# Two paddings of 128 bytes in SBUF, which put the two operands of the large matmuls half of 256 bytes apart

## The chip, the cores and the metric

The kernel runs on one core of one Trainium2 chip. The metric is device time in microseconds (us) for one launch; lower is better. Three runs of the kernel before took 962.54, 964.48 and 963.08 us, with a median of 963.08 us.

## The reference, cut to what matters

Input and output are one sequence of 2048 tokens with 640 channels, in float32. Two blocks follow each other, each with a layer norm whose scale, shift and gate are rows of a small modulation product.

```
mod = silu(c) @ w_mod                      # six rows of 640
h = layernorm(x) * (1 + ca) + sa
x = x + ga * (conv(h, K) + h * Dskip)      # K: 2048 taps per channel, from 192 complex modes
h = layernorm(x) * (1 + cb) + sb
x = x + gb * ((h @ w_gate) * (h @ w_up)) @ w_down   # 640 -> 1536 -> 640
```

The first block is a long convolution, which the kernel computes through Fourier transforms written as matmuls. The second is the gated product, and the change is about its operands.

## The kernel before, in words

The first half, up to about 500 us, builds the taps of the convolution (sine, cosine and exponential tables that VectorE multiplies and TensorE contracts, lines 745 to 760), transforms taps and input (lines 782 to 937), and multiplies the spectra. Its order is written out by hand in the table `SCHED`. Its tiles lie in the pools `pk`, `pk1`, `kconst`, `f16` and `fp`, whose memory is given back when they are done.

The second half is the gated product over four blocks of 512 tokens. It takes the given-back memory for two pools, `wp` from the left end of SBUF and `gp` from the right, in which almost every tile has one place for the whole half. The blocks come in two pairs. In a pair, the products with `w_gate` and `w_up` for two token blocks are formed from sums and differences of operands, so that fewer products are needed (`y_1` to `z_2`, `x_1`, `x_2`), for twelve slices of 128 hidden units. Then `down` (line 1455) multiplies the result with `w_down`, for one token block after the other.

To keep precision, each float32 operand v is split by `hilo` into a high part, which ScalarE rounds to the float32r type, and a low part, which VectorE computes as v minus the high part (line 992). Each product is then three matmuls: high with high, low with high, high with low. So every large matmul has float32r operands.

- Line 1028, in `prod`: the stationary operand (the one that is loaded into the array first) is a block of 128 columns of a weight tile (`wsgh`, `wsgl`, `wth`, `wtl`, `wsuh`, `wsul`); the moving operand is 512 columns of an activation tile (`hh1`, `hl1`, `hh2`, `hl2`, `sh`, `sl`). The program has 1266 of these; line 1162 (`u_gate`) has 30 more of the same form.
- Line 1455, in `down`: here the stationary operand is a block of 128 columns of an activation tile (`sh`, `sl`, `hh2`, `hl2`, or one of the four `e`), and the moving operand is a weight tile's first 384 or last 256 columns (`wsgh`, `wsgl`), in turn. The program has 576 of each.

Each matmul loads its own weights, and the array can take the next weights while the present matmul streams.

Where the tiles lie: every tile of `wp` and `gp` is a multiple of 256 bytes long in each partition, and in the compiled layout every one of them starts 224 bytes past a multiple of 256. Blocks of 128 float32 columns are 512 bytes, 512 columns 2048 bytes, and 384 columns 1536 bytes, so each operand of lines 1028, 1162 and 1455 also starts 224 bytes past a multiple of 256, moving and stationary alike. `wp` is allocated in the order `gbr`, `xb0`, `xb1`, `wga`, `wgb`, `wur`, `wsgh`, `wsgl`, `st0`, `st1`, `hr`, and then `hh1`, `hl1`, `a5` to `a9` and `e`. `gp` is allocated as one list at its opening (lines 1334 to 1338), from low to high addresses: `a10` to `a14`, `s6`, `z`, `s67`, `hh2`, `hl2`, `sh`, `sl`, then `tf`, `wth`, `wtl`, `wsuh`, `wsul`, and other `a` tiles; its upper end is fixed at the end of SBUF. Between the end of `wp` (byte 106208) and the start of `gp` (byte 106464) 256 bytes are free.

`hr` (line 1063) holds small statistics of the layer norm and is used up to column 44 of its 64.

Of the kernel before, what the change touches and what calls it, by code (L numbers as in the profile page):

```python
# [10 lines left out]
F32 = mybir.dt.float32  # L11
# [8 lines left out]
P = 128  # L20
# [109 lines left out]
def tile_kernel(ctx: ExitStack, tc: tile.TileContext, I, out):  # L130
# [49 lines left out]
    def rstd(mv, rs, nm, v, y, ps=None):  # L180

        if ps is not None:
            m = mv.shape[1]
            v, t = ps[:, 0:m], ps[:, 32 : 32 + m]
            V.tensor_scalar(v, mv[:, :, 1], EPS, None, op0=OP.add)
            act(y, v, AF.Sqrt)
            V.reciprocal(rs, y)
            V.tensor_tensor(v, v, rs, op=OP.mult)
            V.tensor_tensor(v, v, rs, op=OP.mult)
            V.tensor_scalar(v, v, -0.5, 1.5, op0=OP.mult, op1=OP.add)  # L190
            V.tensor_tensor(t, v, rs, op=OP.mult)
            V.tensor_tensor(rs, v, rs, op=OP.mult)
            V.scalar_tensor_tensor(nm, t, -1.0, mv[:, :, 0], op0=OP.mult, op1=OP.mult)
            return
        V.tensor_scalar(v, mv[:, :, 1], EPS, None, op0=OP.add)
        act(y, v, AF.Sqrt)
        V.reciprocal(rs, y)
        V.tensor_tensor(y, rs, rs, op=OP.mult)
        V.tensor_tensor(y, y, v, op=OP.mult)
        V.tensor_scalar(y, y, -0.5, 1.5, op0=OP.mult, op1=OP.add)  # L200
        V.tensor_tensor(rs, rs, y, op=OP.mult)
        V.scalar_tensor_tensor(nm, mv[:, :, 0], -1.0, rs, op0=OP.mult, op1=OP.mult)
# [751 lines left out]
    FIRST, SMALL = {}, []  # L954
# [105 lines left out]

    def head_r(tb, st):
        if not SMALL:
            SMALL.append(wp.tile([P, 64], F32, name="hr"))
        mv = SMALL[0][:, 0:8].rearrange("p (i s) -> p i s", s=2)
        rs, nm, rv, ry = (SMALL[0][:, j : j + 4] for j in (16 + 4 * (tb % 2), 24 + 4 * (tb % 2), 32, 40))
        for i in range(4):
            V.bn_aggr(mv[:, i, :], st[:, i])
        rstd(mv, rs, nm, rv, ry)
        HN[tb] = (rs, nm)
# [44 lines left out]
    def u_ln(tb):  # L1114

        st = head_st(tb)
        need(1, "xr", tb, 0)
        head_b(tb, st, range(NB - 2))
        yield
        need(NB - 1, "d", tb)  # L1120
        head_b(tb, st, (NB - 2,))
        yield
        need(NB, "d", tb)
        head_b(tb, st, (NB - 1,))
        head_r(tb, st)
        mark("ln", tb)
        if tb:
            yield
            head_i(1, range(3))
            yield  # L1130
            x, (rs, nm) = XB[1][:, 3, :], HN[1]
            G.tensor_scalar(x, x, rs[:, 3:4], nm[:, 3:4], op0=OP.mult, op1=OP.add)
# [148 lines left out]
    for t in range(3 * NK + 24):  # L1281
        for i in range(3):
            due(3 * t + i)
        if t == 3 * NK + 1:
# [3 lines left out]
            wp = ctx.enter_context(tc.tile_pool(name="wp", bufs=1, reuse_waits="tile"))  # L1288
# [44 lines left out]
    H2, SX = ("hh2", "hl2"), ("sh", "sl")  # L1333
    for n, sh_, dt_, b_ in ([(f"a{j}", [P, 512], F32, 1) for j in range(10, 15)] + [(n, [P, 512], F32, 1) for n in TMP]
                            + [(n, [P, 3, 512], F32R, 1) for n in H2] + [(n, [P, 9, 512], F32R, 1) for n in SX]
                            + [("tf", [P, 8, P], F32, 1), ("wth", [P, 8, P], F32R, 2), ("wtl", [P, 8, P], F32R, 2), ("wsuh", [P, 4, P], F32R, 2),
                               ("wsul", [P, 4, P], F32R, 2)] + [(f"a{j}", [P, 512], F32, 1) for j in (*range(5), *range(15, 24))]):
        FIRST[n] = gp.tile(sh_, dt_, name=n, bufs=b_)
# [167 lines left out]
    def stats(tb, i0):  # L1506
        if i0 == 0:
            ST[tb] = head_st(tb)
        head_b(tb, ST[tb], range(NB), range(i0, i0 + 2))
        if i0:  # L1510
            head_r(tb, ST.pop(tb))
# [113 lines left out]
```

## Time and profile before

| what | before |
|---|---|
| median of three runs | 963.08 us |
| the profiled execution, its own time | 962.99 us |
| its span, from the first to the last instruction | 961.2 us |
| mean granted TensorE clock | 0.975 |
| TensorE matmuls (PE), records and busy time | 11070, 864.6 us |
| weight loads (PEld), records and busy time | 11070, 715.9 us |
| VectorE (DVE), ScalarE (ACT), GpSimd (POOL) busy | 760.1, 569.7, 567.8 us |

The page lists each engine's busy time, then a strip of 40 slices of the span, then the chain of work that ended last. A matmul's record runs from its start to the time its last result is through the pipeline, so records of matmuls that follow each other overlap, and a sum of their durations is more than the time they take. The time that one of them takes in a stream is the distance between starts: the step. The timeline merges neighbouring records of one group; its columns are the start, the time from the first start to the last end, the engine, the line, the tiles (output, then inputs), the shapes and the count.

### The profile page before, as it was taken

To read this page: it belongs to the slowest core of one execution; us is meant where nothing else is said; L and a number is where in the kernel's file an instruction comes from. 1 tells how busy PE (TensorE), PEld (TensorE's weight loads), DVE (VectorE), ACT (ScalarE), POOL (GpSimd) and SP (SyncE) were. 2 spreads that over 40 slices of the span, in tenths; PEclk is the share of its full clock that TensorE was granted. 3 is DMA by queue.
4 is the path that set the end of the run, shared out by engine and by line. 5 is a ranking of instruction groups with operands and counts; after the bars stand their busy time and mean duration, and the time that the engine had idled before them with its cause. 6 is when DMAs were issued, how large, how long until landed. Compare 5 with 4: busy or idle time off the path is not lost.

```text
span 961.2 us, 26424 instructions
## 1 busy us (share of the span) xinstructions
PE 864.6 (90%) x11070; PEld 715.9 (74%) x11070; DVE 760.1 (79%) x1328; ACT 569.7 (59%) x1022; POOL 567.8 (59%) x419
## 2 busy tenths in 40 slices
PE   2778876898798699989889999999999999999998
PEld 1565655676575467678567888899998888889998
DVE  8988678888989988897899877696677877688452
ACT  6889988887987888864773322235555322224330
POOL 5999999799799999950126767631031544451000
PEclk9977999899999889999999999999999999999999
DMA  9487565444565644558953454255536222212241
GB/s 301 152 267 263 150 217 191 134 132 126 145 181 147 186 130 144 161 175 266 254 168 89 130 192 139 80 192 164 193 137 219 84 83 82 83 55 83 83 165 55
DMA packets 141320, 148.94 MB, mean 155 GB/s; under 512 B 8208, under 2 KB 119568, under 8 KB 139792
## 3 DMA queue, kind: packets, MB, share of 16 engines
q1 hardware_dynamic: 139904, 145.80, 48.6%
q8 instruction: 87, 1.43, 0.6%
q10 hardware_dynamic: 1296, 1.44, 0.5%
q14 instruction: 33, 0.27, 0.1%
HBM read 108.36 MB, written 38.86 MB: 153 GB/s over the span
## 4 chain that ended last, share of the span: by engine, by line
PE 49%; DVE 4%; ACT 1%; DMA 1%; issue 1%; DVEq 0%; SPq 0%; ACTq 0%
PE pa L1028 28%; PE pa L1455 17%; PE psg L1028 1%; DMA wga<-B_w_gate 1%; DVE sl L992 1%; PE psg L1108 0%; PE psg L1455 0%; DVE a L1147 0%; PE psg L1162 0%; DVE xb L1468 0%; ACT wsgh L135 0%; PE psfa L887 0%; DVE f16a L873 0%; DVE f16a L874 0%; PE psfb L887 0%
## 5 line engine op out<-in xcount | busy, mean ns | idle before, releaser
L649 POOL TENSOR_TENSOR EQ<-LQ,RH 128x1536 f32<-128x1536 f32 x40 | 124.2, 3106 | 2.2 <-DVE QtB L731 2.1
L135 ACT ACTIVATE z<-pa 128x512 f32<-128x512 f32 x24 | 14.4, 599 | 168.0 <-PE pa L1028 115.0
L992 DVE TENSOR_TENSOR wsgl<-wga,wsgh 128x640 fp32r<-128x640 f32 x72 | 69.8, 973 | 45.6 <-ACT wsgh L135 45.6
L135 ACT ACTIVATE wsgh<-wga 128x640 fp32r<-128x640 f32 x72 | 52.3, 732 | 63.4 <-PE pa L1455 34.1
L1399 POOL TENSOR_TENSOR z<-z,s 128x512 f32<-128x512 f32 x24 | 34.2, 1423 | 88.4 <-DVE s L1398 88.4
L1004 POOL TENSOR_TENSOR tf<-wur,wgb 128x256 f32<-128x256 f32 x24 | 18.8, 784 | 97.0 <-DVE wtl L992 58.9
L649 POOL TENSOR_TENSOR EP<-LP,RH 128x768 f32<-128x768 f32 x40 | 65.7, 1651 | 11.8 <-DVE PtB L731 11.8
L1455 PE MATMUL pa<-wsgh,sh 128*128 128x384 f32 (+1 forms) x295 | 68.6, 311 | 0.0
L1455 PE MATMUL pa<-wsgl,sh 128*128 128x384 f32 (+1 forms) x295 | 68.2, 310 | 0.0
L1455 PE MATMUL pa<-wsgh,sl 128*128 128x384 f32 (+1 forms) x295 | 68.2, 310 | 0.0
L649 POOL TENSOR_TENSOR Pha<-LH,DH 128x1536 int32<-128x1536 int32 (+1 forms) x21 | 62.4, 2971 | 1.8 <-ACT tra L135 1.6
L649 POOL TENSOR_TENSOR Phb<-LH,DH 128x1536 int32<-128x1536 int32 x20 | 62.3, 3113 | 0.0
L992 DVE TENSOR_TENSOR wtl<-tf,wth 128x256 fp32r<-128x256 f32 (+1 forms) x72 | 58.8, 844 | 0.0
L731 DVE TENSOR_TENSOR QtA<-tra,EQ 128x1024 f32<-128x1024 f32 x44 | 51.9, 1215 | 7.7 <-ACT tra L135 4.8
L1397 DVE TENSOR_TENSOR s<-pa,s 128x512 f32<-128x512 f32 x24 | 16.6, 690 | 42.8 <-PE pa L1028 37.8
L731 DVE TENSOR_TENSOR QtA<-trb,EQ 128x1024 f32<-128x1024 f32 x36 | 42.7, 1217 | 9.7 <-ACT trb L135 5.5
L760 PE MATMUL kg<-QtB,PtB 64*32 64x64 f32 x2560 | 46.1, 222 | 4.7 <-issue 2.7
L760 PEld LDWEIGHTS kg<-QtB,PtB 64*32 64x32 f32 x2560 | 39.1, 110 | 12.5 <-issue 6.4
L1028 PE MATMUL pa<-sh,wtl 128*128 128x512 f32 x144 | 44.7, 391 | 0.8 <-DVE wtl L992 0.8
L1455 PEld LDWEIGHTS pa<-wsgh,sl 128*128 128x128 f32 x295 | 45.3, 188 | 0.0
L1455 PEld LDWEIGHTS pa<-wsgl,sh 128*128 128x128 f32 x295 | 45.3, 188 | 0.0
L1455 PEld LDWEIGHTS pa<-wsgh,sh 128*128 128x128 f32 x295 | 45.3, 188 | 0.0
(653 smaller groups left out, 2854.7 us busy)
## 6 DMA issues: line engine op xcount, KB each, us to landing
wga<-wdg SPq DMA_DIRECT2D x24, 640.0 KB, 4.2
wga<-B_w_gate SPq DMA_DIRECT2D x12, 640.0 KB, 5.8
wgb<-B_w_gate SPq DMA_DIRECT2D x24, 320.0 KB, 3.3
wur<-B_w_up SPq DMA_DIRECT2D x24, 320.0 KB, 4.0
xb<-x2d SPq DMA_DIRECT2D x6, 1280.0 KB, 7.1
t_ti<-w_mod SPq DMA_DIRECT2D x3, 1600.0 KB, 9.5
t_tw<-w_mod SPq DMA_DIRECT2D x3, 1600.0 KB, 9.8
WD<-Wa SPq DMA_DIRECT2D x8, 512.0 KB, 4.1
```

Source lines behind the costliest of these rows:

```text
L135: return S.activation(o, i, f, **kw)
L649: G.tensor_tensor(o.rearrange("p x (h l) -> p x h l", l=8), lo.unsqueeze(2).to_broadcast([P, rows, nh, 8]), hi.rearrange("p h x -> p x h") ...
L731: V.tensor_tensor(t, tr, e.unsqueeze(1).to_broadcast([P, 2, R, 32]), op=OP.mult)
L760: PE.matmul(kg[j * 32 : j * 32 + 32, dd, :], PtB[lo : lo + 64, c, r, :], QtB[lo : lo + 64, c, r, :], start=False, stop=dd == 7 and c == 1, ...
L992: V.tensor_tensor(lo, v, hi, op=OP.subtract)
L1004: G.tensor_tensor(t[:, 0:2], u[:, 0:2], g[:, 0:2], op=OP.subtract)
L1028: PE.matmul(ps, w[a][:, k], x[b][:, l], start=n == 0 and m == 0, stop=n == 2 and m == len(ks) - 1)
L1397: V.tensor_tensor(S67[i], ps, S6[i], op=OP.add)
L1399: G.tensor_tensor(ZT[i], ZT[i], S67[i], op=OP.add)
L1455: PE.matmul(ACC[tb][t][c], x[:, ts], w[:, cs], start=st, stop=f == NF - 1 and n == 2 and (one or t % 2 == 1))
```

## The change: what it does

`hr` becomes 96 columns wide, that is 384 bytes instead of 256, and a tile `gap` of 128 bytes, which nothing reads or writes, is put between `sl` and `tf` in the list of `gp`. No instruction is added, removed or moved.

```
     def head_r(tb, st):
         if not SMALL:
-            SMALL.append(wp.tile([P, 64], F32, name="hr"))
+            SMALL.append(wp.tile([P, 96], F32, name="hr"))
...
     for n, sh_, dt_, b_ in ([(f"a{j}", [P, 512], F32, 1) for j in range(10, 15)] + [(n, [P, 512], F32, 1) for n in TMP]
                             + [(n, [P, 3, 512], F32R, 1) for n in H2] + [(n, [P, 9, 512], F32R, 1) for n in SX]
+                            + [("gap", [P, 32], F32, 1)]
                             + [("tf", [P, 8, P], F32, 1), ("wth", [P, 8, P], F32R, 2), ("wtl", [P, 8, P], F32R, 2), ("wsuh", [P, 4, P], F32R, 2),
```

By the order of allocation, the tiles of `wp` behind `hr` (`hh1`, `hl1`, `a5` to `a9`, `e`) move up by 128 bytes, and the tiles of `gp` ahead of `gap` (`a10` to `a14`, `s6`, `z`, `s67`, `hh2`, `hl2`, `sh`, `sl`) move down by 128. All of these then start 96 bytes past a multiple of 256. The weight tiles and the rest stay at 224. The 256 free bytes are used up.

More of the change, by code (lines that the diff above doesn't have):

```diff
@@ L1062, in head_r @@
         if not SMALL:
-            SMALL.append(wp.tile([P, 64], F32, name="hr"))
+            SMALL.append(wp.tile([P, 96], F32, name="hr"))
         mv = SMALL[0][:, 0:8].rearrange("p (i s) -> p i s", s=2)
@@ L1335, in tile_kernel @@
                             + [(n, [P, 3, 512], F32R, 1) for n in H2] + [(n, [P, 9, 512], F32R, 1) for n in SX]
+                            + [("gap", [P, 32], F32, 1)]
                             + [("tf", [P, 8, P], F32, 1), ("wth", [P, 8, P], F32R, 2), ("wtl", [P, 8, P], F32R, 2), ("wsuh", [P, 4, P], F32R, 2),
```

## The prediction

> **What bounds the kernel now.** I read the page's head and its chain of waits first, then the chain in order of time, then busy time by stretch, and last the timeline of PE and of its weight loads (PEld) at single steps.
>
> ```profile
> span 961.2 us, 26424 instructions
> PE 49%; DVE 4%; ACT 1%; DMA 1%; issue 1%; DVEq 0%; SPq 0%; ACTq 0%
> PE pa L1028 28%; PE pa L1455 17%; PE psg L1028 1%; DMA wga<-B_w_gate 1%; DVE sl L992 1%; PE psg L1108 0%; PE psg L1455 0%; DVE a L1147 0%; PE psg L1162 0%; DVE xb L1468 0%; ACT wsgh L135 0%; PE psfa L887 0%; DVE f16a L873 0%; DVE f16a L874 0%; PE psfb L887 0%
> ```
> ```profile
> 507.43 124.95 PE pa L1028 x549
> 636.46 45.76 PE pa L1455 x312
> 728.97 139.73 PE pa L1028 x615
> 872.78 45.05 PE pa L1455 x307
> ```
> ```profile
> 500.00:961.20 461.20, 455.70 (x2432) 405.41 (x2430) 329.87 (x526) 164.69 (x319) 171.85 (x157) 1.00 0.38 122
> ```
> ```profile
> engine line waited for: us in total, times, longest us
> PE pa L1028 <- DVE wtl L992: 0.8, 1, 0.8
> PE pa L1028 <- DVE s L1385: 0.8, 1, 0.8
> ```
>
> From 507 us on, the chain runs through matmuls of lines 1028 and 1455, nearly without a break. In the third fence the columns behind the window and its length are busy time of PE, PEld, DVE, ACT and POOL, then the granted clock. PE is busy for 455.70 of 461.20 us at full clock, DVE for 329.87. The last fence, PE's waits from 500 to 961 us, has 1.6 us in all. So this half is bound by how soon one large matmul follows another, and the change can act only through that step: everything it moves is an operand of these matmuls or of an engine with slack.
>
> The step, from the timeline of PE, and under it that of the loads:
>
> ```profile
> 849.95 0.62 PE L1028 MATMUL pa<-sh,wtl 128*128 128x512 f32 x2
> 850.40 0.62 PE L1028 MATMUL pa<-sl,wth 128*128 128x512 f32 x2
> 850.86 0.61 PE L1028 MATMUL pa<-hh,wth 128*128 128x512 f32 x2
> 851.31 0.39 PE L1028 MATMUL pa<-hh,wsuh 128*128 128x512 f32 x1
> 851.54 0.61 PE L1028 MATMUL pa<-hh,wtl 128*128 128x512 f32 x2
> 851.99 0.39 PE L1028 MATMUL pa<-hh,wsul 128*128 128x512 f32 x1
> ```
> ```profile
> 850.63 0.41 PEld L1028 LDWEIGHTS pa<-hh,wth 128*128 128x128 f32 x2
> 851.09 0.19 PEld L1028 LDWEIGHTS pa<-hh,wsuh 128*128 128x128 f32 x1
> ```
> ```profile
> 879.83 0.28 PE L1455 MATMUL pa<-wsgh,sh 128*128 128x256 f32 x1
> 879.95 0.45 PE L1455 MATMUL pa<-wsgh,sl 128*128 128x384 f32 x2
> ...
> 883.76 0.46 PE L1455 MATMUL pa<-wsgl,sh 128*128 128x384 f32 x2
> ```
>
> Nine matmuls of 512 columns start between 849.95 and 851.99 us: 2.04/9 = 226.7 ns each. The load for the matmul at 851.31 begins at 851.09, together with the matmul before it (the second of the row 850.86), so the next weights are read while the present columns stream. In line 1455 thirteen pairs of 384 and 256 columns start between 879.95 and 883.76 us: 3.81/13 = 293 ns a pair, of which the 256 columns take some 120 (879.83 to 879.95).
>
> What a stream costs where operands are plain float32 stands in the modulation product, line 285:
>
> ```profile
> 98.79 1.67 PE L285 MATMUL psfa<-t_tw,sil 128*128 128x256 f32 x7
> ```
> ```profile
> L285 PE MATMUL psfb<-t_ti,sil x10: 379/379/379, 31.9 to 33.9; 128*128 128x256 f32 x10
> ```
>
> Seven matmuls in 1.67 us with 0.38 us for the last give (1.67 - 0.38)/6 = 215 ns per step. Plain float32 takes about twice as long a column as float32r (215 against 120 ns for 256 columns), so these 256 columns are as long a stream as 512 in float32r. The float32r matmul takes 226.7 - 215 = 11.7 ns more. That excess is all that there is to gain.
>
> **The change, part by part.** Instructions, counts and queues stay. The `hr` padding and `gap` cost nothing to execute: no work touches the added bytes. In the compiled layout, moved tiles cross no edge of a tile of the earlier half, so the reuse of that memory brings each tile the same predecessors and no new wait: 0 us.
>
> What moves is the distance between operands: 0 modulo 256 before, 128 after, in 1240 recorded matmuls of line 1028 in this half and 1152 of line 1455:
>
> ```profile
> 500.00:961.20 461.20, 282.24 (x1240) 231.81 (x1238) 1.00 0.38 122
> ```
> ```profile
> 500.00:961.20 461.20, 171.32 (x1152) 169.29 (x1152) 1.00 0.38 122
> ```
>
> The first of these is line 1028 alone, the second line 1455. The trace has no float32r matmul with another distance, so the price is bounded. At the best, the excess goes entirely: 1240 x 11.7 ns = 14.5 us, and in line 1455, where 640 columns at 215/512 ns are 269 ns, 576 x (293 - 269) ns = 13.8 us. That is 28 us, or 935 us; with a few ns for the second start of each pair and waits that come up in place of PE, I put it at 25 us, or 938. On the other side, nothing in the rows excludes that the new distance is the worse one; its price is in the rivals.
>
> Which end is nearer? The excess could be the load of the next weights getting in the way of the moving columns when both begin at the same place modulo 256. Then a matmul without a load beside it should be free of it. The trace has such a one: timeline from 502 us, PE first, then PEld, and the single record from a narrower window.
>
> ```profile
> 502.63 0.61 PE L1028 MATMUL pa<-sh,wth 128*128 128x512 f32 x2
> 504.07 0.73 PE L1028 MATMUL pa<-sh,wtl 128*128 128x512 f32 x2 [0.82 <-DVE wtl L992]
> ```
> ```profile
> 502.63 0.19 PEld L1028 LDWEIGHTS pa<-sh,wth 128*128 128x128 f32 x1
> 504.07 0.30 PEld L1028 LDWEIGHTS pa<-sh,wtl 128*128 128x128 f32 x2 [1.25 <-DVE wtl L992]
> ```
> ```profile
> 502.86 0.39 PE L1028 MATMUL pa<-sh,wth 128*128 128x512 f32 x1
> ```
>
> The matmul at 502.86 has no load beside it until 504.07, when it has long ended. It still takes 0.39 us, as the ones at 851.31 and 851.99 do with a load beside them, and not the 0.379 of the equally long float32 stream. So the excess is there without the neighbour that the change moves away. Ends of matmuls are partly modelled in the profile, which is why I do not take this as final.
>
> Two more rows show that distance is not what separates steps with and without excess:
>
> ```profile
> 408.66 0.39 PE L827 MATMUL psfc<-ghc,t_tw 128*64 128x128 f32 x4
> 408.87 0.39 PE L827 MATMUL psfb<-ghc,t_tw 128*64 128x128 f32 x4
> 409.09 0.39 PE L827 MATMUL psfc<-ghc,t_tw 128*64 128x128 f32 x4
> ```
> ```profile
> 717.02 1.03 PE L1108 MATMUL psg<-ident,xb 128*128 128x128 f32 x8
> ```
> ```profile
> L1108 PE MATMUL psg<-ident,xb x40: 271/273/328, 682.1 to 721.7; 128*128 128x128 f32 x40
> ```
>
> Line 827 has float32 operands at distance 0 modulo 256 (both tiles start 192 past a multiple, and both slices are multiples of 256 bytes); its matmuls, two at a time in two halves of the array, come four in 0.215 us ((409.09 - 408.66)/2), 108 ns a pair: 215/2 for half the columns, no excess. The transposes of line 1108 have distance 160 (`ident` at 128, `xb` at 224) and come every (1.03 - 0.27)/7 = 109 ns, also without. Both distances are free of it; the float32r type is what the steps with excess share. I therefore take the lower end, no effect of the distance.
>
> [...]
>
> The sum: the profiled execution took 962.99 us, 1.8 outside its span of 961.2, and lies 0.09 below the median of the three runs (963.08). 962.99 + 0 gives **963.0 us**. A measurement of this kernel can tell about 0.2%, 1.9 us, from no change.
>
> **The rivals.** *The reads collide, and the distance of 128 ends it.* For it: every float32r step of the half has the excess, at every distance that is 0 modulo 256, and it is constant (226.7 ns over whole stretches: 139.73 us/615 = 227), as a fixed pattern of addresses would make it; plain float32, which asks for half as many columns per ns, may just leave room. Against it: the lone matmul. Whole, it gives 936 to 941; in part, for instance on line 1028 alone or half of each excess, 948 to 960. PE would have to step 6% faster, and DVE at 329.87 of then 435 us could still follow.
>
> *The new distance slows the loads, and the 256-column steps become bound by them.* In line 1455 a load of 128 columns has only the step of 256 columns, some 120 ns, to hide in. What a load needs at least, from loads beside matmuls of a single column:
>
> ```profile
> L304 PEld LDWEIGHTS psfb<-ident,TVa x16: 181/187/187, 51.4 to 54.2; 1*128 1x128 f32 x16
> L304 PEld LDWEIGHTS psfb<-ident,TVb x14: 187/187/187, 52.5 to 54.6; 1*128 1x128 f32 x14
> ```
>
> Thirty loads from 51.4 to 54.6 us: 110 ns each. It decides from about 10 ns more per load (the 120 is rounded, so from 5 to 15); if a load grew by the 11.7 ns by which the stream is longer now, the pair would grow by up to 7 ns, say 5: 576 x 5 = 3 us, 966 us. For it: PEld is busy 169.29 us of PE's 171.32 in line 1455, so there is little slack. Against: nothing shows that a load feels a distance at all. If line 1028 suffered too it would be more, which no row prices.
>
> *The change does not take effect as described*, because the pool lays its tiles otherwise. Then nothing moves apart and the time is 963 too.
>
> **How the numbers follow.** No effect of the distance, 0.54, with the layout rival (0.02) in it; reads that collide and are parted, 0.33, of which 0.2 whole (936 to 941) and 0.13 in part; slower loads, 0.13. The likeliest case's own range is 961.5 to 964.5. Cases of one sign don't hold most of the chance, so the range takes in the whole-gain case from its middle, 937, up to 966 for the slower one. What is left out is the better half of the whole gain and a slowdown beyond the price above. Faster by over 0.2%: 0.33; within: 0.54; slower: 0.13.
>
> **What would show it right or wrong.** Right: nine 512-column matmuls still take 2.04 us, the pair of line 1455 still 293 ns, the chain's first long stretch 125 us for 549, and the lone matmul before the wait for `wtl` 0.39 us. Wrong towards faster: a step near 215 ns in line 1028, and a span shorter after 500 us only; if line 1028 speeds up and 1455 does not, the partial case. Wrong towards slower: pairs of 298 ns or more with line 1028 unchanged, or a load longer than 188 ns. A difference ahead of 480 us would refute all of it, since nothing there has moved.

## The result, and the profile after

The change makes the kernel slower by three quarters of a per cent: 969.28 us (median of six runs, 968.11 to 972.24) against 962.0 (six runs, 961.01 to 964.48), a ratio of 1.0075 with a 95% interval of 1.0056 to 1.0094. The profiled execution took 968.81 us.

The head of the page of after:

```profile
span 967.0 us, 26424 instructions
```

The chain in order of time, after (start, length, what; line 1455 is now 1456):

```profile
506.26 127.84 PE pa L1028 x549
638.28 44.74 PE pa L1456 x312
729.62 142.99 PE pa L1028 x615
876.78 46.07 PE pa L1456 x307
```

The chain has the same four long stretches with the same counts. Nothing is lost ahead of them: the first begins 1.2 us earlier than before. But the same 549 matmuls take 127.84 us in place of 124.95, and the same 615 take 142.99 in place of 139.73, which is 5.3 ns more for each. Line 1455 went both ways: 312 matmuls took 1.0 us less than before, 307 took 1.0 us more. The step itself stands in the timeline of PE. These are the same nine matmuls of the program as in the prediction's rows, which here begin 3.4 us later:

```profile
853.38 0.62 PE L1028 MATMUL pa<-sh,wtl 128*128 128x512 f32 x2
853.84 0.64 PE L1028 MATMUL pa<-sl,wth 128*128 128x512 f32 x2
854.32 0.62 PE L1028 MATMUL pa<-hh,wth 128*128 128x512 f32 x2
854.78 0.39 PE L1028 MATMUL pa<-hh,wsuh 128*128 128x512 f32 x1
855.01 0.62 PE L1028 MATMUL pa<-hh,wtl 128*128 128x512 f32 x2
855.47 0.40 PE L1028 MATMUL pa<-hh,wsul 128*128 128x512 f32 x1
```

Nine matmuls start between 853.38 and 855.47 us: 2.09/9 = 232 ns, against 226.7. Matched one by one in program order, the mean step of line 1028 is 232.4 ns after and 226.9 before (the 1256 steps that hold no wait).

Busy time from the first matmul of line 1028 to the last matmul of the kernel, after and then before (window, length, busy PE, PEld, DVE, ACT, POOL, granted clock):

```profile
492.40:962.80 470.40, 468.51 (x2457) 411.63 (x2458) 333.42 (x534) 170.16 (x329) 171.99 (x157) 1.00 0.38 122
```
```profile
493.60:957.00 463.40, 461.78 (x2457) 410.53 (x2458) 335.20 (x534) 170.22 (x329) 171.85 (x157) 1.00 0.38 123
```

The same 2457 records of PE need 470.40 us in place of 463.40, at a clock of 1.00 in both. Of these 7.0 us, 6.7 are PE's own busy time, while that of the other engines hardly moved. The 1256 matched steps of line 1028 add up to 7.0 us (5.5 ns each), the size of the whole loss; what line 1455 gained and lost nearly cancels. PE's longest waits after:

```profile
PE pa L1028 <- DVE s L1386: 0.8, 1, 0.8
PE pa L1028 <- DVE wtl L992: 0.7, 1, 0.7
PE psg L1108 <- ACT xb L135: 0.5, 1, 0.5
```

The first two are those of before; the third, 0.5 us once, is new. PE's idle time in the two windows is 1.9 us after and 1.6 before, so waits explain 0.3 us at most. Each 512-column matmul is followed 5.5 ns later by the next.

### The profile page after: what moved, and what is told of

Read it like the earlier page. It is cut to its first block, busy times and chain, and to the rows that moved or that the text cites. A ratio compares the mean times of both kernels' runs of the same rounds, so it can differ in the third digit from the quotient of the medians.

```text
span 967.0 us, 26424 instructions
## 1 busy us (share of the span) xinstructions
PE 870.6 (90%) x11070; PEld 717.7 (74%) x11070; DVE 758.4 (78%) x1328; ACT 569.6 (59%) x1022; POOL 567.7 (59%) x419
## 4 chain that ended last, share of the span: by engine, by line
PE 48%; DVE 5%; ACT 1%; issue 1%; DMA 1%; SPq 0%; DVEq 0%; ACTq 0%
PE pa L1028 28%; PE pa L1456 15%; PE psg L1028 1%; DVE st L1081 1%; PE psg L1162 1%; DVE sl L992 1%; DMA TVb<-WD 1%; PE psg L1108 0%; PE psg L1456 0%; DVE a L1147 0%; ACT hh L135 0%; ACT xb L135 0%; DVE xb L1469 0%; DVE wsgl L992 0%; PE psfa L887 0%
```

## The experiments

**Theory A:** what counts is how the moving operand lies to the stationary one, modulo 256 bytes; both are read while a stream runs, and 128 apart is the worse distance. **B:** what counts is the place of one tile alone (96 instead of 224). **C:** the moved tiles meet other engines' accesses, and a stream by itself would not feel the distance. Distance is from here on the start of the moving operand minus that of the stationary one, modulo 256. Where the table below names a kernel by its distance, that is line 1028's; in line 1455 the roles are exchanged, so its distance is 192 where line 1028 has 64, and the other way round.

To compare kernels whose first half varies by some us from run to run, I take the time in the profile from the start of the chain's first long stretch to the end of its last one: before, 872.78 + 45.05 - 507.43 = 410.4 us; after, 416.6.

**All operands moved alike.** The activations lie at 96 modulo 256 as in the change, the weights too, so the distance is 0 again. The lead tile is allocated ahead of everything else in `wp`, and the gap stands last in the list of `gp`.

```
+    wp.tile([P, 32], F32, name="lead")
     gbr = mk("gbr", [P, D])
...
+    ... + [("gap", [P, 32], F32, 1)]      # at the end of gp's list
```

> All tiles of both pools 128 bytes further, weights too: every operand of the large matmuls starts 96 past a multiple of 256, at distance 0 from the other. If the distance between the two operands sets the step (theory A), all is as before: 512-column steps of 226.7 ns, pairs of line 1455 at 293 ns, about 962 us. If the place of the activations sets it (theory B, 96 worse than 224), steps stay near 232 ns and the time near 969 us. If the loss came from elsewhere (theory C), nothing is said.

Its chain:

```profile
509.18 124.95 PE pa L1028 x549
638.21 45.76 PE pa L1457 x312
730.67 139.74 PE pa L1028 x615
874.50 45.05 PE pa L1457 x307
```

The four lengths are those of before to 0.01 us; the sum is 410.4. The time is 962.03 us, a ratio of 0.9988 (0.9965 to 1.0012). B falls: every activation lies where the change put it and costs nothing there. What the change moved is a distance.

**One of the two paddings, and two other distances.** With `hr` alone widened, only `hh1`, `hl1` and `e` (and scratch) move. With its width and that of `gap` divided otherwise, the distance is 64 or 192.

```
hr [P, 96], no gap            # hh1, hl1, e at distance 128, the rest at 0
hr [P, 80],  gap [P, 48]      # distance 64
hr [P, 112], gap [P, 16]      # distance 192
```

> Only the padding of hr: hh1, hl1 and e move by 128 bytes, the rest of the activations stays at distance 0. Theories A and B: within one run, 512-column steps on hh1 and hl1 (360 of 1296) at 232 ns and all others at 226.7 ns, and the pairs of line 1455 on e (the first two of twelve slices) off 293 ns; about 1.9 us from the 360 matmuls, so 963 to 965 us. Theory C: steps alike on all activations.

> hr padded by 64 and gap of 192 bytes: activations 64 past the weights modulo 256 (the free 256 bytes split otherwise). Theory A: a third value of the step, between the floor of 215 ns and 240; if the two reads meet less at a quarter of 256, below 226.7 ns and under 962 us. Theory B: a value of its own too, for the place 32. If neither distance nor place matters, 226.7 ns.

> hr padded by 192 and gap of 64 bytes: activations 192 past the weights, that is 64 ahead of them, modulo 256. Theory A: as in the run at distance 64 if only the size of the distance counts; otherwise the sign shows, with line 1028 and line 1455 (where the roles are exchanged) going opposite ways. Theory B: a value of its own for the place 160.

| kernel | step of line 1028, ns | long stretches, us | ratio (95%) |
|---|---|---|---|
| `hr` alone | 232.4 on `hh1`, `hl1`; 227.6 on the others | 412.5 | 1.0009 (0.9988 to 1.0029) |
| distance 64 | 229.3 | 413.2 | 1.0018 (0.9997 to 1.0040) |
| distance 192 | 233.3 | 418.0 | 1.0076 (1.0050 to 1.0103) |

Within one kernel, `hr` alone makes the steps longer whose moving operand was moved, and a few behind them. The 227.6 hides that: the first three steps behind each of the 34 stretches on `hh1` and `hl1` take 231.4 ns in the mean, though both of their operands lie at distance 0, and the later ones 227.1. One such place in the timeline:

```profile
521.41 0.63 PE L1028 MATMUL pa<-hh,wth 128*128 128x512 f32 x2
...
522.57 0.39 PE L1028 MATMUL pa<-hh,wsul 128*128 128x512 f32 x1
...
523.25 0.39 PE L1028 MATMUL pa<-hl,wsuh 128*128 128x512 f32 x1
```

The product that begins at 521.41 follows one on `hh1` and `hl1`; its own operand `hh2` was not moved. Its first five steps take 1.16/5 = 232 ns, the next three 0.68/3 = 227. So a step also depends on what ran before it, and not on its own two operands alone.

The two time ratios whose interval holds 1 say nothing by themselves; the steps in the trace do. And the price is no simple function of the distance: half way, at 64, it is less than half of the price at 128, and at 192 it is higher still. The sign counts too, in both lines: where line 1455 has distance 192 (the kernel with 64), its two long stretches take 46.80 and 44.03 us, which is 300 and 287 ns a pair; where it has 64 (the kernel with 192), 45.76 and 45.06, as before.

**The streams by themselves.** A kernel that computes nothing of the reference and hands its input on as output: 48 matmuls with a new weight block each, seven PSUM banks in turn, no other engine at work, one stream for each of sixteen distances; then streams of 256 columns, pairs of 384 and 256, plain float32, two places of the weights in turn, and chains whose last matmul has no load beside it.

```
for a in range(16):
    for i in range(48):
        PE.matmul(bank(), W(i), x[a][:, 4 * a : 4 * a + 512], start=True, stop=True)
```

> A kernel that computes nothing of the reference (its output is the input): streams of float32r matmuls with no other engine at work, 48 per distance, moving operand 0 to 240 bytes past the stationary ones modulo 256 in steps of 16 (512 columns), of 32 (256 columns, and 384 with 256 in turn), a control in plain float32, streams whose stationary operands alternate between two places, and matmuls alone or as the last before a wait. Theory A (reads of one matmul and of the next load meet): the step follows the distance: 226.7 at 0, about 229 at 64, 232 at 128, 233 at 192 as in the whole kernel, without any other engine; plain float32 stays at 215 ns; with stationary places in turn the step follows the place of the next load; a lone matmul is free of it at every distance. If other engines' reads were part of it, the steps here would be nearer 215 at every distance.

The timeline of PE, first matmul of a stream and first of the next, so that the difference over 48 is the step; `ma` is distance 0, `mb` 16, `mi` 128, `mj` 144, `mm` 192, `mn` 208, `mp` 240:

```profile
34.07 0.39 PE L60 MATMUL pf<-ma,wr 128*128 128x512 f32 x1
44.95 0.39 PE L60 MATMUL pe<-mb,wr 128*128 128x512 f32 x1
...
122.85 0.40 PE L60 MATMUL pe<-mi,wr 128*128 128x512 f32 x1
134.01 0.39 PE L60 MATMUL pd<-mj,wr 128*128 128x512 f32 x1
...
167.65 0.39 PE L60 MATMUL pa<-mm,wr 128*128 128x512 f32 x1
178.84 0.39 PE L60 MATMUL pg<-mn,wr 128*128 128x512 f32 x1
...
201.30 0.40 PE L60 MATMUL pe<-mp,wr 128*128 128x512 f32 x1
212.19 0.28 PE L63 MATMUL pd<-ma,wr 128*128 128x256 f32 x1
370.29 0.38 PE L70 MATMUL pa<-fa,wf 128*128 128x256 f32 x1
380.65 0.38 PE L70 MATMUL pd<-fe,wf 128*128 128x256 f32 x1
391.01 0.38 PE L70 MATMUL pg<-fi,wf 128*128 128x256 f32 x1
401.37 0.38 PE L70 MATMUL pc<-fm,wf 128*128 128x256 f32 x1
```

At distance 0: 10.88/48 = 226.7 ns; at 128: 11.16/48 = 232.5; at 192: 11.19/48 = 233.1; at 240: 10.89/48 = 226.9. These are the steps of before, of the change and of the kernel with 192, without any other engine: C falls. The other distances take 229 (64), 231 (80 and 112), and 232 to 235 (the rest, 235 at 208); none is below distance 0. Four things more. The last rows are plain float32, where each of the 24 matmuls of a stream leaves two records: 10.36/48 = 216 ns at distance 0, 64 and 128 alike, and 215.8 at 192, so plain float32 of 256 columns took the same time at these four distances. Streams of 256 columns in float32r take 118 to 120 ns at all eight distances tried, 120 at distance 0. The pairs take 293 ns at 0, 64, 96, 160 and 224, 291.5 at 32, 287 at 128 and 300 at 192. And the last matmul of a chain, with no load beside it, has 0.39 or 0.40 us at 0, 64, 128 and 192 at full clock. The weights' place in turn did not give two alternating steps, as was expected: with the moving operand at one place and the weights at 0 and 128 in turn, nearly every step takes 232 to 235 ns, also those whose own or next weights are at distance 0; with 0 and 64 in turn, four steps of 226, 236, 232 and 226 ns repeat.

**More of the same streams.** Other lengths at distance 0, distances under 16 bytes, and two places in turn, 0 and 64 or 0 and 128, either so that each moving operand is at distance 0 from its own weights, or from the weights of the next matmul, which are loaded while it streams (in the first streams the load for the matmul at 484.53 us begins at 484.31, beside the matmul of 484.30).

```
PE.matmul(bank(), W(i, e*(i%2)), x[i%2][:, e*(i%2)     : e*(i%2) + 512], ...)      # own
PE.matmul(bank(), W(i, e*(i%2)), x[i%2][:, e*(1-i%2)   : e*(1-i%2) + 512], ...)    # next
```

> Again streams alone. Other column counts at distance 0 (512 down to 320): if the 11 ns over the plain float32 stream are a fixed cost per matmul, the step falls by 0.417 ns per column; if a stream can only follow the one before it at certain instants (theory D), it stays at 226.7 for some counts and then falls in jumps. Distances of 4 to 24 and -4 to -24 bytes: near 0 the step stays 226.7 if the 16 bytes of the last sweep are the grain. Both operands' places in turn (0 and 64, 0 and 128): with each matmul at distance 0 from its own weights, or from the next ones. Theory A with the next load: 226.7 only where the next distance is 0; with the own weights: only where the own distance is 0; theory D: in neither, since the place changes from one stream to the next. Last, twenty pairs of 384 and 256 columns, eight times after different beginnings, at distances 0 and 128: at 0 always 293.5 ns a pair; at 128 either 286.6 or 300, by the beginning.

```profile
33.53 0.39 PE L60 MATMUL pf<-ma,wr 128*128 128x512 f32 x1
44.41 0.39 PE L60 MATMUL pe<-mb,wr 128*128 128x508 f32 x1
...
116.83 0.33 PE L60 MATMUL pe<-mi,wr 128*128 128x384 f32 x1
125.15 0.32 PE L60 MATMUL pd<-mj,wr 128*128 128x352 f32 x1
...
346.73 0.34 PE L75 MATMUL pc<-mi,wr 128*128 128x384 f32 x1
...
347.93 0.34 PE L75 MATMUL pd<-mi,wr 128*128 128x384 f32 x1
...
353.77 0.33 PE L75 MATMUL pc<-mi,wr 128*128 128x384 f32 x1
...
354.91 0.33 PE L75 MATMUL pd<-mi,wr 128*128 128x384 f32 x1
```

In the timeline 512 columns take 10.88/48 = 226.7 ns and 384 take 8.32/48 = 173.3; 320 take 146.7. That is (226.7 - 146.7)/192 = 0.417 ns a column and 13.3 ns beside it, while 352, 416 and 448 columns have 14 to 16 ns beside it. Nor does the step fall evenly just under 512: 508 and 504 columns take 227.7 and 226.6 ns, 500 and 496 both 223.3. So what is beside the columns is no fixed cost; jumps of this kind were expected if a stream can follow the one before it only at certain instants (theory D above), but they do not prove it. Distances of 4 and 244 are among the worst (237 and 240 ns). The simple form of A, that a load and a stream collide as pairs, falls here: with own or next weights at distance 0, places in turn still take 228 to 233 ns, more than 226.7 in all four arrangements. The last four rows are the same pairs at distance 128, entered twice: four pairs take 1.20 us (300 ns each) the first time and 1.14 (287) the second. Of eight entries five settled at 287 and three at 300; at distance 0 all eight took 293. The eight are four beginnings (none to three matmuls of 256 columns ahead of the pairs), each run twice: three of the four came out alike both times, and the one with three matmuls ahead once at 287 and once at 300. So the program's entry alone does not fix the outcome.

**The length of the load.** If a load's reads delayed the stream, a short load would cost less.

```
PE.matmul(bank()[0:m], W(i)[:, 0:m], x[...], ...)           # m = 128, 96, 64, 32 at distance 0, 128, 192
PE.matmul(bank(), wr[:, 128*i : 128*i+1].to_broadcast([P, P]), x[...], ...)   # a load that reads one column
```

> Streams alone, 512 columns, with stationary operands of 128, 96, 64 and 32 columns at distances 0, 128 and 192; and loads of 128 columns that all read one and the same column. Theory A (the reads of loads and of moving columns meet): what a step has over 213.3 ns falls with the length of the load, to a quarter or so at 32 columns, at every distance, and nearly vanishes where the load reads one column alone. If the 13.3 ns at distance 0 belong to the float32r stream itself, they stay at every length, and only the 6 ns that distance 128 adds may fall. If nothing of it is in the load, 226.7, 232.5 and 233.3 at every length.

```profile
33.39 0.39 PE L60 MATMUL pf<-ma,wr 128*128 128x512 f32 x1
44.27 0.39 PE L60 MATMUL pe<-mb,wr 128*96 128x512 f32 x1
55.32 0.39 PE L60 MATMUL pd<-mc,wr 128*64 128x512 f32 x1
...
88.61 0.39 PE L63 MATMUL pa<-mf,wr 128*96 128x512 f32 x1
99.50 0.39 PE L63 MATMUL pg<-mg,wr 128*64 128x512 f32 x1
...
166.04 0.40 PE L69 MATMUL pa<-mm,wr 128*128 128x512 f32 x1
177.16 0.40 PE L69 MATMUL pg<-mn,wr 128*128 128x512 f32 x1
```

At distance 0 the full load gives 226.7 ns and the one of 96 columns 11.05/48 = 230; at distance 128 the load of 96 columns gives 10.89/48 = 226.9, where the full load gives 232. Loads that read one column only (last two rows) give 11.12/48 = 231.7 at distance 0, 64, 128 and 192 alike. The step does not fall with the length of the load: at distance 0 each shorter load takes more than the full one, at 128 and 192 each takes less, and with 32 columns the three distances give 231.7, 230.6 and 231.7. With loads of 32 columns, or of one column read again and again, the effect of the distance is nearly or wholly gone and the step is near 231.7. Distance 0 with full loads is 5 ns below that, a favourable case and not one with the effect taken away.

**The better distance for each line.** Line 1028 at distance 0, line 1455 at 128, where pairs can settle at 287 ns: the tiles of `wp` up to `hl1` move to 96, `e` and all of `gp` stay at 224. (At some 66 steps of line 1028, where a product on weights of one pool follows one on weights of the other, the next weights lie at another distance.) The change ran again beside it on the same chip, and the mixed kernel was measured once more later.

```
+    wp.tile([P, 32], F32, name="lead")
     gbr = mk("gbr", [P, D])
...
     HX[0] = mk("hh1", ...), mk("hl1", ...)
+    wp.tile([P, 32], F32, name="gap")
```

> Distance 0 for every matmul of line 1028 and 128 for every one of line 1455 (wp's tiles up to hl1 moved by 128, the rest in place). 512-column steps as before, 226.7 ns; pairs of line 1455 at 286.6 or 300 ns in each of the two stretches of 288 pairs, as the entry has it: 286.6 in both gives 4 us less than before (958), 300 in both 4 us more (966), one of each no change (962). So the loss of the change is in line 1028: some 7 us of its 7 are gone here.

> The change once more, for a second profile: 512-column steps again 232.4 ns in the mean, and if the pairs of line 1455 settle by the entry alone, again 286.6 in the first stretch and 300 in the second; if by chance, another mix. About 969 us.

> The same kernel as in the mixed run, for more runs: as its pairs settle at 286.6 or 300 ns by chance, between 957 and 966 us, in the median 1 to 2 us under before.

The chain of the change again, and then of the mixed kernel in its second run:

```profile
510.88 128.37 PE pa L1028 x549
643.44 46.79 PE pa L1456 x312
736.82 142.99 PE pa L1028 x615
883.99 46.07 PE pa L1456 x307
```
```profile
505.08 125.26 PE pa L1028 x549
634.42 44.74 PE pa L1457 x312
725.64 140.04 PE pa L1028 x615
869.76 44.05 PE pa L1457 x307
```

The change took 972.73 us, a ratio of 1.0121 (1.0094 to 1.0148), more than the first time: here both stretches of line 1455 settled at 300 ns a pair (46.79/156), where one of the two had settled at 287 in its first profile (44.74/156). That is 2.1 of the 2.6 us by which its long stretches grew (419.2 against 416.6). In the mixed kernel line 1028 takes 0.3 us more than before in each stretch, and both stretches of line 1455 are 1.0 us shorter, 287 ns a pair, in both profiles. Its long stretches take 408.7 us in both, against 410.4. From the first matmul of line 1028 to the last of the kernel it takes 460.9 us in both, 2.5 less than before (463.4); 576 pairs times 6.7 ns would be 3.9 us, of which line 1028 gives a part back. The times: 961.1 us and 0.998 (0.9958 to 1.0001), then 958.7 and 0.9966 (0.9942 to 0.9989). The second interval lies below 1, the first just reaches it, so the gain over before is shown by the traces and only just by the times. Against the change the gain is plain: measured side by side, 961.1 and 972.7 us.

## Why the prediction was wrong

The prediction said 963.0 us, with a range from 937 to 966; measured were 969.28.

*What bounds the kernel* held: the half is one matmul after another, and nearly all of the loss is a longer step, behind 490 us; waits are 0.3 us of it. That the two paddings run nothing held too, and the layout rival fell, since the step changed, and went back when the weights were moved along.

*The step that failed* is "I therefore take the lower end, no effect of the distance", the 0 in "962.99 + 0". In its place the runs show 232.4 ns a step against 226.9, 7.0 us in all. It rested on two readings. First, the lone matmul: at 502.86 us it took 0.39 us without a load beside it, as others do with one. After, it reads

```profile
501.84 0.40 PE L1028 MATMUL pa<-sh,wth 128*128 128x512 f32 x1
```

and in the streams it is 0.39 to 0.40 at 0, 64, 128 and 192. The reading was true and beside the point: a record's length (0.39 us) is how long one matmul is under way, its end partly modelled, and the kernel's price is how soon the next may start (0.227 us). At most the lone matmul says that what a float32r matmul takes beyond plain float32 is not all due to a neighbour; that the neighbour's distance changes nothing doesn't follow. Second, the rows "free of it" at distances 0 and 160, lines 827 and 1108, were plain float32, whose 256 columns in the streams take 215.8 to 216 ns a record at four distances. They cannot say what float32r does. The prediction itself wrote that the trace has no float32r matmul with another distance. A row of another type was used as if the distance were all that varied.

*The other end of the bound*, 215 ns, was not there either: "That excess is all that there is to gain" took plain float32 as the floor, where in the streams each of 24 matmuls left two records of some 216 ns. Float32r at 512 columns was never below 226.7 ns at any distance tried, and from 320 to 512 columns 13.3 ns beside the columns is the least. Shorter ones come closer: 256 columns at 117.8 ns have 11, and the pairs at 287 have 10 for each of the two. The kernel before was already at the best distance for line 1028, so the faster rival had no gain to give; only line 1455 had one, of 6.7 ns a pair, and not reliably from the change: its two profiles show stretches at 287 and at 300.

*The slower rival* had the sign but neither the place nor the price. It expected loads to grow and the pairs of line 1455 to pay 3 us. The loads of both lines stay at 188 ns, and the long stretches of pairs came out at about 0 and 2 us in the two profiles. The loss is in the case named last, "If line 1028 suffered too it would be more, which no row prices": 5.5 ns a step, 7.0 us. With no row for it, a bound of the same size as the gain (11.7 ns a step, 14 us) would have been the honest upper end; 966 was the price of one mechanism.

That the distance itself matters is shown by the streams: 226.7 against 232.5 ns by nothing but the distance of the two operands, with no other engine at work. Which read waits for which, if any does, is not shown.

*What is shown and what stays open.* Shown: the relative place changes the step of a long stream (226.7 ns at 0, 232.5 at 128; all operands moved alike: the stretches of before to 0.01 us), with some steps of delay behind a switch (231.4 ns for the first three, then 227.1), no other engine is needed, float32r of 512 columns feels it, plain float32 of 256 columns does not (215.8 to 216 ns a record at four distances). Not shown is how. That a load's reads collide one by one with the stream's is contradicted by the short loads (230 ns with 96 columns at distance 0, 226.7 with 128) and by the places in turn (228 to 233 ns), and the one-column loads (231.7 ns at four distances) and the long steps behind `hh1` do not fit it. The stream with the weights at 0 and 64 in turn settled in a repeating pattern (226, 236, 232, 226 ns), and the pairs at distance 128 in one of two states (287 or 300 ns), which would fit a phase between the reads of the loads and the stream that is carried from one matmul to the next; the trace has no record of the reads themselves, so this remains a guess.

## What to carry to other kernels

Here the operands' distance modulo 256 was worth 7.0 us (232.4 against 226.9 ns a step). Where a stream of float32r matmuls bounds a kernel, the addresses can be treated as a parameter like any other: try a few distances by padding, for each shape of matmul, and judge by start to start in the timeline, over a stretch of hundreds. Before taking a row as evidence that something has no effect, see that it has the same type and shape, and that it measures the quantity in the sum. Where no row prices one direction, keep that end of the range as wide as the other.

## What was not expected of the hardware

- In the streams by themselves the step of a 512-column float32r matmul changed with the operands' distance modulo 256 bytes: 226.7 ns at 0, 240 and 252; 229 at 12, 64 and 236; 230 to 235 at most others; 240 at 244. Differences showed within 16 bytes (237 at 4, 229 at 12).
- It also changed with what ran before: in the kernel with `hr` alone widened, behind products at distance 128, three to five more steps at distance 0 took 231 to 232 ns in the mean before the stream was back at 227.
- Pairs of 384 and 256 columns settled at 287, 293 or 300 ns (291.5 at distance 32) and stayed there for the rest of a stream; at distance 128 they settled at 287 five times and at 300 three times of eight, and the same kernel had a stretch at 287 in one run and at 300 in the other.
- Loads of fewer columns slowed one stream and sped up another: 96 columns in place of 128 took it from 226.7 to 230 ns at distance 0, and from 232 to 227 at distance 128.
